# Smaller first loads, transposes in groups of six, thirteen raw rows and a two-piece last store in a fused layernorm and MLP

## The chip, the cores and the metric

The kernel runs on one core of a Trainium2 chip. The metric is the device time in microseconds of one execution. An execution is also profiled once; times within it are counted from the start of its span.

## The reference

```python
def reference(x, w1, b1, w2, b2):            # x [1, 2048, 1024], w1 [1024, 3584], w2 [3584, 1024], all bf16
    y = _layernorm(x, axis=-1)
    h = _gelu(jnp.einsum("bsd,df->bsf", y, w1) + b1)
    return jnp.einsum("bsf,fd->bsd", h, w2) + b2
```

Each of the 2048 tokens is normalised over its 1024 features (mean removed, divided by the root of the variance plus 1e-5), multiplied by w1, given b1 and a tanh gelu, multiplied by w2 and given b2.

## The kernel before

**Tiling.** The tokens are cut into 16 tiles of 128, four tiles to a block of 512 (`TB`), so there are four blocks. The first product is made transposed: a *row* r is 128 of the 3584 columns of w1 (28 rows, `FT`), and a row's result is a PSUM tile of 128 partitions by 512 tokens, summed over eight contraction blocks (`DT`). One matmul of a row and a contraction block is a *cell* (`pe_cell`, L415). A gelu on ScalarE (`act_gelu`, L424) takes the row from PSUM to `hT_sb`. The second product (`out_chunk`, L467) makes 128 tokens by 512 output columns as a sum of 28 matmuls; VectorE adds b2 (L478) and SP stores the piece. For each block TensorE runs the 28 rows and then eight output chunks.

**PSUM.** There are eight banks: `ps_t` (one bank, for transposes and for rows), `ps_1` (five banks, for rows) and `ps_2` (two, for the first rows, then for output chunks). `new_unit` gives a row its bank. Rows 0 to 6 of block 0 take 1_0 to 1_4, 2_1, 2_0; all later rows go round t, 1_0, 1_1, 1_2, 1_3, 1_4. The first cell in a bank waits for the gelu that last read the bank.

**Block 0 before its statistics are known.** The cells need the tokens transposed. For later blocks VectorE normalises and transposes (`ops_norm`, `ops_T`). For block 0 tiles 0 to 2 (`N_RAW`) are transposed on TensorE as they are (`pe_T`, L383), copied by ScalarE from PSUM to `yT_sb` (L391), and rows 0 to 6 (`R`, the *wave*) run on these raw values. A column of ones behind the 384 raw tokens (`RC`) gives the sum of each row's weights. VectorE takes the statistics (`op_stats`, L271, two halves of 512 features to a tile; `op_aggr`, L279), GpSimd the power -1/2 (L276, L498), and VectorE turns means and inverse roots into rows (`ops_rows`, L283 to L290; `ops_rvt`, L294) that TensorE spreads over the partitions (`pe_row`, L564) and ScalarE copies out (L567). `act_cs` (L531) copies the weight sums. VectorE then corrects each wave row in PSUM in two operations (`ops_corr`: `sa_r`, L540, and `sb_r`, L543). Tile 3 is normalised by VectorE before it is transposed on TensorE, and enters the wave rows as late cells of 128 columns (`late_cells`).

From row 7 on, the rows of block 0 use tokens that VectorE has *centred* (`ops_fix`, L339, one operation a tile, needing the row of means), 512 columns at a time, and VectorE only multiplies them by the inverse root (`dve_scale`, L548). In row 7 the last tile's 128 columns come first and the 384 behind them.

**Order.** Each engine runs its instructions in the order in which the program lists them. `_emit` puts a wait on a semaphore ahead of an instruction for each event it needs. The orders of TensorE and ScalarE are written by hand for the wave; VectorE's list begins with `head` (statistics, rows, norm of tile 3, b1, the three centrings), then the corrections, and the rest is merged from two lists: `crit` (work on PSUM, taken in the order it was appended) and `fill` (preparation of the next blocks), by estimated times that begin at `T_PE_START` and `T_DVE_START`.

**Loads.** SP issues `SP_FIRST_LOADS` and then all other loads; ScalarE issues `ACT_FIRST_LOADS` ahead of its table load. w0 to w7 are the eight contraction blocks of w1 for rows 0 to 6 (224 KB each), w8 and up the further rows. x0a, x1a and x2a are the first 512 features of a tile, xrb the other 512 of tiles 0 to 2. At the start TensorE runs `WARM` matmuls on constants (L491).

**End.** The last half tile of output is made in four pieces of 128 columns (`TAIL_PIECES`), each with its own add and store.

Of the kernel before, what the change touches and what calls it, by code (L numbers as in the profile page):

```python
# [18 lines left out]
TAIL_PIECES = 4  # L19
WARM = 24  # L20
N_RAW = 3
RC = N_RAW * P
HALVES = (0, 4, 8)
W1_CHUNK_COLS = (512, 512, 1024, 640)
N_W2_CHUNKS = 4
SP_FIRST_LOADS = ("x0a", "w0", "w1", "xrb", "w2", "w3", "w4", "x3a", "x3b", "w5", "w6", "w7", "b1", "w8")
ACT_FIRST_LOADS = ("x1a", "x2a")

T_PE_START = 4.2
T_DVE_START = 26.0  # L30
# [54 lines left out]
def bass_standalone__mixer_channel_mlp__prompt_kernel(  # L85
# [23 lines left out]
    assert HALVES[-1] == DT and 0 < N_RAW < TPB  # L109
# [27 lines left out]
    with ExitStack() as es:  # L137
# [25 lines left out]
        cs_sb = sb("cs_sb", [P, R], F32)  # L163
# [44 lines left out]
        def issue(item):  # L208
            if item == "xrb":
                dma(x_sb[:, 0:N_RAW, HC:D], xf[0:N_RAW * P, HC:D].rearrange("(t p) d -> p t d", p=P), item,  # L210
                    N_RAW * P * HC * 2)
                for i in range(N_RAW):
                    x_ev[i] = (f"x{i}_0", item)
            elif item[0] == "x" and item[-1] in "ab":
                i, h = int(item[1:-1]), "ab".index(item[-1])
                dma(x_sb[:, i, h * HC:(h + 1) * HC], xf[i * P:(i + 1) * P, h * HC:(h + 1) * HC], f"x{i}_{h}",
                    P * HC * 2)
                x_ev[i] = (f"x{i}_0", f"x{i}_1")
# [15 lines left out]
        for i in range(TPB):  # L234
            if i not in x_ev:
                load_x_tile(i)
            else:
                for h, evn in enumerate(x_ev[i]):
                    if evn not in est:
                        issue(f"x{i}" + "ab"[h])  # L240
# [29 lines left out]
        def op_stats(i, h):  # L270
            return (lambda e, i=i, h=h: e.bn_stats(st_sb[:, i, 6 * h:6 * (h + 1)], x_sb[:, i, h * HC:(h + 1) * HC]),  # L271
                    [x_ev[i][h]], f"st{i}_{h}", 0.65)
# [64 lines left out]
        def ops_fix(i):  # L337
            s0, s1 = i * P, (i + 1) * P
            return [(lambda e: e.tensor_tensor(out=yT_sb[:, 0, :, s0:s1], in0=yT_sb[:, 1, :, s0:s1],  # L339
                                               in1=row_sb[:, 0:1, s0:s1].to_broadcast([P, DT, P]), op=ALU.add),  # L340
                     ["row0", f"te{i}_0", f"te{i}_1"], f"fx{i}v", 1.25)]
# [4 lines left out]
        def ops_T(i):  # L346
            blk, t = divmod(i, TPB)
            waits = [y_ev[i][-1]]
            if blk - 2 in mm1_done:
                waits.append(mm1_done[blk - 2])  # L350
            elif blk == 1:
                waits += [f"cw_{R - 1}"] + list(FX)
# [13 lines left out]

        pe_t = [T_PE_START]
        bank_read = {}
        t_bank = {"t": ps_t[:, 0, :], "2_0": ps_2b[:, 0, :], "2_1": ps_2b[:, 1, :]}

        def pe_T(parts, bname):
            bap = t_bank[bname]
            nb = HALVES[1]
            last = f"tp{parts[-1][0]}_{parts[-1][1]}"
            w0 = ["ident"] + ([bank_read[bname]] if bname in bank_read else [])
            copies = []
            for n, (i, k) in enumerate(parts):
                j0, j1 = HALVES[k], HALVES[k + 1]
                buf, s0 = (1 if i < N_RAW else 0), i * P
                o = n * nb * P  # L380
                for j in range(j0, j1):
                    waits = (w0 if n == 0 else []) + [x_ev[i][k] if i < N_RAW else y_ev[i][j]] if j == j0 else []
                    pe.op(lambda e, i=i, j=j, o=o + (j - j0) * P: e.transpose(  # L383
                        out=bap[:, o:o + P], in_=x_sb[:, i, j * P:(j + 1) * P], identity=ident[:, :]),
                        waits=waits, sig=(f"tp{i}_{k}" if j == j1 - 1 else None))
                    yT_ev.setdefault(i, [None] * DT)[j] = f"te{i}_{k}"
                src = bap[:, o:o + (j1 - j0) * P].rearrange("p (j s) -> p j s", j=j1 - j0)
                copies.append((yT_sb[:, buf, j0:j1, s0:s0 + P], src, f"te{i}_{k}"))
                pe_t[0] += (j1 - j0) * 0.056
            for dst, src, sig in copies:  # L390
                act.op(lambda e, dst=dst, src=src: e.copy(out=dst, in_=src), waits=[last], sig=sig)  # L391
                bank_read[bname] = sig
# [104 lines left out]
        head = [op_stats(i, h) for h in range(2) for i in raw] + [op_aggr(i) for i in raw]  # L497
# [3 lines left out]
        head += [op_stats(N_RAW, 0), op_stats(N_RAW, 1), op_aggr(N_RAW)] + ops_rows() + ops_rvt() + ops_norm(N_RAW)  # L501
        for i in range(N_RAW + 1, TPB):
            head += [op_stats(i, 0), op_stats(i, 1), op_aggr(i)] + ops_norm(i)
        head += ops_b1()
        h = DT // 2
        FX = [f"fx{i}v" for i in raw]
        for i in raw:
            head += ops_fix(i)
        for o in head:
            dve_put(o)  # L510

# [15 lines left out]
        cs_ap, cs_ev, corr = {}, {}, []  # L527
# [10 lines left out]
        def ops_corr(r):  # L538
            ap = unit_bank(wave[r][0])[:, 0:RC + 1]
# [11 lines left out]

        def late_cells(t, rows, dts):
            for r in rows:
                for dt in dts:
                    last = t == TPB - 1 and dt == DT - 1
                    pe_cell(r, dt, 0, t * P, (t + 1) * P, wave[r][0], [cs_ev[r], yT_ev[t][dt]],
                            f"m1_0_{r}" if last else None, False, last, shared=True)
                    if last:
                        corr.extend(ops_corr(r))
                        act_gelu(r, 0, TPB, wave[r][0], f"sb_{r}", f"g_0_{r}")  # L560
                        hT_row[(0, r)] = f"g_0_{r}"
# [9 lines left out]

        first, most, every = range(NB1), [*range(NB1), R - 1], range(R)
        pe_T([(0, 0)], "t")
        pe_T([(1, 0)], "2_0")
        cells(first, (0,), 0, 1)
        pe_T([(2, 0)], "2_1")
        cells(first, (0,), 1, 2)
        cells((R - 1,), (0,), 0, 2)
        cells(most, (1,), 0, 2)
        cells((NB1,), (0, 1), 0, 2)  # L580
        pe_T([(0, 1), (1, 1)], "t")
        cells(every, (0, 1), 2, 3)
        cells(every, (2,), 0, 3)
        pe_T([(2, 1)], "t")
# [3 lines left out]
        cells(first, (DT - 1,), 0, 3)
        act_cs(ps_1, 0, NB1, False)
        last2 = range(NB1, R)  # L590
        cells(last2, (4,), 0, 3)
        pe_T([(3, 0), (3, 1)], "t")
        cells(last2, range(5, DT), 0, 3)
        act_cs(ps_2, NB1, R, True)
        r4 = R // 2 + 1
        late_cells(3, range(r4), range(h))
        pe_row(1)
        late_cells(3, range(r4), range(h, DT))
        late_cells(3, range(r4, R), range(DT))
        for o in corr:  # L600
            dve_put(o)

        def mm1_rows(b, r0):
            for r in range(r0, FT):
                mm1_row(b, r, ((N_RAW, TPB), (0, N_RAW)) if b == 0 and r == r0 else ((0, TPB),))

        mm1_rows(0, R)
        for b in range(NB):
# [11 lines left out]
            for st in range(TPB):  # L620
                for dh in range(DH):
# [4 lines left out]
                    if last and TAIL_PIECES > 1:  # L626
                        pw = NCH // TAIL_PIECES
                        for k in range(TAIL_PIECES):
                            out_chunk(b, st, c0 + k * pw, c0 + (k + 1) * pw, dh if k == 0 else f"{dh}p{k}", prev)
# [65 lines left out]
```

## Time and profile before

| what | value |
|---|---|
| median of 3 runs | 397.79 us (397.51 to 397.87) |
| profiled execution | 397.62 us, span 396.36 us |
| granted TensorE clock (mean of the records) | 1.000 |
| TensorE busy | 393.4 us (99%) |
| VectorE, ScalarE busy | 160.6 us (41%), 83.4 us (21%) |
| second product (L467) | 980 matmuls, 194.3 us |
| first product (L415) | 979 matmuls, 167.3 + 34.0 us |
| transposes on TensorE (L383) | 32 matmuls |

A line of the timeline has the start in us, the length in us, the engine, the line of the code, the operation, written tile <- read tiles, the shape and the number of instructions merged into it; in brackets the idle time before it and what ended it. The chain that ended last is followed back from the last instruction through whatever released each step. Matmuls overlap, so their pace is read from the distance of their starts.

### The profile page before, as it was taken

The page shows a single profiled execution, that of the slowest core. Times are in us where ns is not written, and L with a number is a line of the kernel's source. Part 1 is how long each engine was busy: PE and PEld are TensorE (multiplying, and loading weights), DVE is VectorE, ACT ScalarE, POOL GpSimd, SP SyncE. Part 2 cuts the span into 40 slices and gives each one's busy share as a digit, 9 for nine tenths or more (in the row PEclk, how much of TensorE's full clock was granted, in tenths as well). Part 3 has the DMA queues.
Part 4 walks back from the last instruction along what each step waited for, and adds up shares of the span by engine and source line. Part 5 has one row for each costly group of instructions (what it writes and reads, how often), then busy time and mean ns, then how long its engine had stood idle before and what let it go on. Part 6 is the DMA issues. An engine that isn't in the chain of part 4 may idle for free.

```text
span 396.4 us, 4688 instructions
## 1 busy us (share of the span) xinstructions
PE 393.4 (99%) x2017; PEld 187.8 (47%) x2017; DVE 160.6 (41%) x340; ACT 83.4 (21%) x125; POOL 9.8 (2%) x28
## 2 busy tenths in 40 slices
PE   8999999999999999999999999999999999999998
PEld 7744444444444444444444444444444444444447
DVE  5988889988999405987100000001100000001111
ACT  4373330000143342000023443100003334400000
POOL 2001100011000100000000000000000000000000
PEclk9999999999999999999999999999999999999999
DMA  7999940000000000000000000000000000000001
GB/s 272 361 378 386 387 155 13 28 26 14 28 0 0 2 0 2 27 14 27 26 13 2 0 0 2 13 13 28 21 20 13 0 2 0 0 15 26 13 28 28
DMA packets 17036, 23.64 MB, mean 60 GB/s; under 512 B 1656, under 2 KB 10744, under 8 KB 17016
## 3 DMA queue, kind: packets, MB, share of 16 engines
q1 hardware_dynamic: 16728, 23.08, 16.5%
q8 instruction: 16, 0.26, 0.3%
q10 hardware_dynamic: 288, 0.26, 0.2%
q14 instruction: 4, 0.03, 0.0%
HBM read 19.14 MB, written 4.19 MB: 59 GB/s over the span
## 4 chain that ended last, share of the span: by engine, by line
PE 98%; DMA 1%; SPq 0%; DVE 0%; issue 0%
PE ps L467 49%; PE ps L415 41%; PE ps_t L415 8%; DMA w_sb<-in_w_dram 1%; PE ps_t L383 0%; SPq L185 0%; PE ps_t L564 0%; DVE o_sb L478 0%
## 5 line engine op out<-in xcount | busy, mean ns | idle before, releaser
L467 PE MATMUL ps<-w_sb,hT_sb 128*128 128x512 bf16 (+1 forms) x980 | 194.3, 361 | 0.0
L415 PE MATMUL ps<-yT_sb,w_sb 128*128 128x512 bf16 (+4 forms) x827 | 167.3, 360 | 0.3 <-ACT yT_sb L391 0.3
L467 PEld LDWEIGHTS ps<-w_sb,hT_sb 128*128 128x128 bf16 x980 | 91.1, 98 | 102.8
L415 PEld LDWEIGHTS ps<-yT_sb,w_sb 128*128 128x128 bf16 x827 | 77.6, 98 | 85.5 <-ACT yT_sb L391 0.5
L424 ACT ACTIVATE hT_sb<-ps,b_sb 128x512 bf16<-128x512 f32 x94 | 64.4, 687 | 234.6 <-PE ps L415 217.2
L478 DVE TENSOR_TENSOR o_sb<-ps,b_sb 128x512 bf16<-128x512 f32 (+1 forms) x35 | 22.6, 646 | 198.3 <-PE ps L467 198.2
L359 DVE STREAM_TRANSPOSE yT_sb<-x_sb 32x256 bf16<-32x256 bf16 x192 | 83.7, 436 | 21.6 <-PE ps_t L415 18.6
L415 PE MATMUL ps_t<-yT_sb,w_sb 128*128 128x512 bf16 (+2 forms) x152 | 34.0, 368 | 0.0
L271 DVE BATCH_NORM_STATS2 st_sb<-x_sb 128x6 f32<-128x512 bf16 x32 | 21.1, 676 | 4.1 <-DMA x_sb<-in_x_dram 3.9
L415 PEld LDWEIGHTS ps_t<-yT_sb,w_sb 128*128 128x128 bf16 x152 | 14.5, 98 | 16.5
L424 ACT ACTIVATE hT_sb<-ps_t,b_sb 128x512 bf16<-128x512 f32 x18 | 12.4, 686 | 17.7 <-PE ps_t L415 14.6
L548 DVE TENSOR_TENSOR ps<-ps,row_sb 128x384 f32<-128x384 f32 x17 | 9.4, 565 | 4.7 <-PE ps L415 4.5
L276 POOL TENSOR_TENSOR rstd_sb<-mv_sb,nhalf 128x1 f32<-128x1 f32 x13 | 7.0, 542 | 116.1 <-DVE mv_sb L279 115.5
L299 DVE TENSOR_SCALAR x_sb<-x_sb,mv_sb,rstd_sb 128x1024 bf16<-128x1024 bf16 x13 | 7.0, 541 | 1.9 <-POOL rstd_sb L276 1.3
L540 DVE SCALAR_TENSOR_TENSOR ps<-row_sb,cs_sb,ps 128x385 f32<-128x385 f32 x7 | 4.3, 615 | 0.0
L391 ACT COPY yT_sb<-ps_t 128x512 bf16<-128x512 bf16 x6 | 3.3, 588 | 4.3 <-PE ps_t L383 4.3
L543 DVE TENSOR_TENSOR ps<-ps,row_sb 128x385 f32<-128x385 f32 x7 | 4.0, 567 | 0.2
L279 DVE BATCH_NORM_AGGREGATE mv_sb<-st_sb 128x2 f32<-128x15 f32 x16 | 3.3, 214 | 1.2
L339 DVE TENSOR_TENSOR yT_sb<-yT_sb,row_sb 128x1024 bf16<-128x1024 bf16 x3 | 3.5, 1222 | 0.1
L491 PE MATMUL ps<-const-bfloat16-1.0 128*128 128x128 bf16 x24 | 2.7, 309 | 0.8 <-PEq L680 0.8
L491 PEld LDWEIGHTS ps<-const-bfloat16-1.0 128*128 128x128 bf16 x24 | 2.5, 143 | 0.8 <-issue 0.8
L548 DVE TENSOR_TENSOR ps_t<-ps_t,row_sb 128x384 f32<-128x384 f32 x4 | 2.3, 564 | 0.9 <-PE ps_t L415 0.8
(36 smaller groups left out, 16.6 us busy)
## 6 DMA issues: line engine op xcount, KB each, us to landing
w_sb<-in_w_dram SPq DMA_DIRECT2D x4, 1792.0 KB, 18.2
out_dram<-o_sb SPq DMA_DIRECT2D x31, 128.0 KB, 1.7
x_sb<-in_x_dram SPq DMA_DIRECT2D x3, 1024.0 KB, 14.5
w_sb<-in_w_dram SPq DMA_DIRECT2D x2, 1024.0 KB, 8.5
w_sb<-in_w_dram SPq DMA_DIRECT2D x1, 2048.0 KB, 14.6
w_sb<-in_w_dram SPq DMA_DIRECT2D x8, 224.0 KB, 5.1
w_sb<-in_w_dram SPq DMA_DIRECT2D x1, 1280.0 KB, 15.9
x_sb<-in_x_dram SPq DMA_DIRECT2D x3, 128.0 KB, 5.0
```

The costliest lines, as they stand in the source:

```text
L271: return (lambda e, i=i, h=h: e.bn_stats(st_sb[:, i, 6 * h:6 * (h + 1)], x_sb[:, i, h * HC:(h + 1) * HC]), [x_ev[i][h]], f"st{i}_{h}", 0.65)
L276: pool.op(lambda e, i=i: e.tensor_tensor(out=rstd_sb[:, i:i + 1], in0=mv_sb[:, i, 1:2], in1=nhalf[:, i:i + 1], op=ALU.pow), waits=[f"mv{i} ...
L299: return (lambda e, i=i, c0=c0, c1=c1: e.tensor_scalar(out=x_sb[:, i, c0:c1], in0=x_sb[:, i, c0:c1], scalar1=mv_sb[:, i, 0:1], scalar2=rst ...
L359: res.append((lambda e, src=src, dst=dst: e.transpose(out=dst, in_=src), waits, (f"tr{i}" if lastop else None), 0.47))
L415: pe.op(lambda e: e.matmul(unit_bank(bank)[:, n0:n1], lhsT=w1_sb[:, dt, r * P:(r + 1) * P], rhs=yT_sb[:, buf, dt, n0:n1], start=start, sto ...
L424: act.op(lambda e, r=r, n0=n0, n1=n1, bank=bank: e.activation(out=hT_sb[:, r, n0:n1], in_=unit_bank(bank)[:, n0:n1], func=ACT.Gelu_apprx_tanh,
L467: pe.op(lambda e, st=st, ft=ft, c0=c0, c1=c1, bank=bank: e.matmul(ps_2[:, bank, 0:c1 - c0], lhsT=hT_sb[:, ft, st * P:(st + 1) * P], rhs=w2 ...
L478: crit.append((est[sig], (lambda e, ob=ob, c0=c0, c1=c1, bank=bank: e.tensor_tensor(out=o_sb[:, ob, c0:c1], in0=ps_2[:, bank, 0:c1 - c0], ...
L491: pe.op(lambda e: e.matmul(ps_1[:, 0, 0:P], lhsT=unit, rhs=unit, start=True, stop=True), waits=[gate] if gate else [])
L540: return [(lambda e: e.scalar_tensor_tensor(out=ap, in0=row_sb[:, 0, :], scalar=cs_ap[r], in1=ap, op0=ALU.mult, op1=ALU.add), [f"m1_0_{r}" ...
L543: (lambda e: e.tensor_tensor(out=ap, in0=ap, in1=row_sb[:, 1, :], op=ALU.mult), [f"sa_{r}", "row1"], f"sb_{r}", 0.56)]
L548: crit.append((est[wait_ev], (lambda e: e.tensor_tensor(out=ap, in0=ap, in1=row_sb[:, 1, 0:RC], op=ALU.mult), [wait_ev, "row1"], f"sc_{r}" ...
```

## The change

- First loads: x0p, x1p, x2p bring the first 256 features of tiles 0 to 2 (two contraction blocks); xq brings features 256 to 511 of the three tiles and xr the other 512. w0 is now issued by ScalarE, ahead of x2p. Tile 3 comes in one load.
- TensorE: 20 warm matmuls, three fillers (`FILL`) between the transposes of tile 0 and tile 1; the first two blocks are transposed a tile at a time, the other six blocks for the three tiles together, six transposes to a group, with one ScalarE copy of 384 columns for each block. Block 0 of the contraction runs a tile at a time, the others 385 columns at once.
- Rows 7 to 12 run on the raw tokens as well (`raw_row`): 385 columns, then 128 late columns behind the next raw row; they are corrected with the two operations of `ops_corr`, and their weight sums are copied one by one. Row 13 is now the first centred row, in two parts, with row 12's late cells between.
- VectorE: tile 3's statistics and norm come ahead of the rows of means; the three centrings stand behind the corrections of rows 3, 4 and 5. The gelus and the weight-sum copies of these rows are put on ScalarE in the order of estimated times.
- The last half tile of output is made in pieces of 384 and 128 columns.

```diff
-TAIL_PIECES = 4
-WARM = 24
+TAIL_PIECES = (384, 128)
+WARM = 20
+FILL = 3
+RAW_ROWS = 13
+CENTRE_BEHIND = (3, 4, 5)
-SP_FIRST_LOADS = ("x0a", "w0", "w1", "xrb", "w2", "w3", "w4", "x3a", "x3b", "w5", "w6", "w7", "b1", "w8")
-ACT_FIRST_LOADS = ("x1a", "x2a")
+SP_FIRST_LOADS = ("x0p", "x1p", "w1", "xq", "w2", "w3", "xr", "w4", "x3", "w5", "w6", "w7", "b1", "w8")
+ACT_FIRST_LOADS = ("w0", "x2p")
...
-        head = [op_stats(i, h) for h in range(2) for i in raw] + [op_aggr(i) for i in raw]
+        head = [op_stats(i, k) for k in range(2) for i in raw]
+        for i in range(N_RAW, TPB):
+            head += [op_stats(i, 0), op_stats(i, 1), op_aggr(i)]
+        head += [op_aggr(i) for i in raw]
...
-        head += [op_stats(N_RAW, 0), op_stats(N_RAW, 1), op_aggr(N_RAW)] + ops_rows() + ops_rvt() + ops_norm(N_RAW)
...
+        for i in range(N_RAW, TPB):
+            head += ops_norm(i)
+        head += ops_rows() + ops_rvt() + ops_b1()
...
-        for i in raw:
-            head += ops_fix(i)
...
+                        for o in ops_corr(r):
+                            crit.append((est[f"m1_0_{r}"], o, 0))
+                            t_corr[0] += o[3]
+                        act_late.append((t_corr[0], lambda r=r: act_gelu(r, 0, TPB, row_bank[r], f"sb_{r}", f"g_0_{r}")))
+                        bank_gelu[row_bank[r]] = hT_row[(0, r)] = f"g_0_{r}"
+                        if r in CENTRE_BEHIND:
+                            for o in ops_fix(CENTRE_BEHIND.index(r)):
+                                crit.append((est[f"m1_0_{r}"], o, 0))
+                                t_corr[0] += o[3]
...
+        def raw_row(r):
+            bank, uw = new_unit()
+            row_bank[r] = bank
+            for dt in range(DT):
+                pe_cell(r, dt, 1, 0, RC + 1, bank, (uw if dt == 0 else []) + [yT_ev[i][dt] for i in range(N_RAW)],
+                        f"cw_{r}" if dt == DT - 1 else None, dt == 0, False, shared=True)
+            cs_ap[r], cs_ev[r] = cs_sb[:, r:r + 1], f"cs_{r}"
+            act_late.append((est[f"cw_{r}"], lambda: act.op(
+                lambda e: e.copy(out=cs_sb[:, r:r + 1], in_=unit_bank(bank)[:, RC:RC + 1]), waits=[f"cw_{r}"],
+                sig=f"cs_{r}")))
...
+        pe_T([(0, 2, 0, 1)], "t")
+        warm(FILL)
+        pe_T([(0, 2, 1, 2)], "2_0")
+        cells(every, (0,), 0, 1)
+        pe_T([(0, 2, 2, 3)], "t")
+        cells(every, (0,), 1, 2)
+        cells(every, (0,), 2, 3)
+        pe_T([(2, 3, 0, 3), (3, 4, 0, 3)], "t")
+        cells(every, (1, 2), 0, 3)
+        pe_T([(4, 5, 0, 3), (5, 6, 0, 3)], "t")
+        cells(every, (3,), 0, 3)
+        cells(first, (4,), 0, 3)
+        pe_T([(6, 7, 0, 3), (7, 8, 0, 3)], "t")
+        cells(last2, (4,), 0, 3)
+        cells(every, (5,), 0, 3)
+        cells(first, (6, 7), 0, 3)
+        act_cs(ps_1, 0, NB1, False)
+        pe_T([(0, 4, 3, 4), (4, 8, 3, 4)], "t")
+        cells(last2, (6, 7), 0, 3)
+        act_cs(ps_2, NB1, R, True)
+        late_row(0)
+        late_row(1)
+        pe_row(0)
+        late_row(2)
+        late_cells(TPB - 1, (3,), range(DT // 2))
+        pe_row(1)
+        late_cells(TPB - 1, (3,), range(DT // 2, DT))
+        for r in range(4, R):
+            late_row(r)
...
+        for r in range(R, NR):
+            raw_row(r)
+            if r > R:
+                late_row(r - 1)
+        mm1_row(0, NR, ((N_RAW, TPB), (0, N_RAW)), between=lambda: (late_row(NR - 1), flush_act()))
+        mm1_rows(0, NR + 1)
```

More of the change, by code (lines that the diff above doesn't have):

```diff
@@ L18 @@
 NOB = 2
-TAIL_PIECES = 4
-WARM = 24
+TAIL_PIECES = (384, 128)
+WARM = 20
+FILL = 3
 N_RAW = 3
+RAW_ROWS = 13
+CENTRE_BEHIND = (3, 4, 5)
 RC = N_RAW * P
-HALVES = (0, 4, 8)
 W1_CHUNK_COLS = (512, 512, 1024, 640)
 N_W2_CHUNKS = 4
-SP_FIRST_LOADS = ("x0a", "w0", "w1", "xrb", "w2", "w3", "w4", "x3a", "x3b", "w5", "w6", "w7", "b1", "w8")
-ACT_FIRST_LOADS = ("x1a", "x2a")
-T_PE_START = 4.2
-T_DVE_START = 26.0
+SP_FIRST_LOADS = ("x0p", "x1p", "w1", "xq", "w2", "w3", "xr", "w4", "x3", "w5", "w6", "w7", "b1", "w8")
+ACT_FIRST_LOADS = ("w0", "x2p")
+T_PE_START = 4.27
+T_DVE_START = 17.5
 DMA_T0 = 2.1
@@ L108, in bass_standalone__mixer_channel_mlp__prompt_kernel @@
     assert NB1 + NB2 + 1 <= 8 and NB2 == 2
-    assert HALVES[-1] == DT and 0 < N_RAW < TPB
+    assert DT == 8 and 0 < N_RAW < TPB
+    QC = 2 * P
+    NR = max(R, min(RAW_ROWS, FT - 2))
     w1_chunks = [(j, j + 1, 0, R * P) for j in range(DT)]
@@ L162, in bass_standalone__mixer_channel_mlp__prompt_kernel @@
         row_sb = sb("row_sb", [P, 2, RC + 1], F32)
-        cs_sb = sb("cs_sb", [P, R], F32)
+        cs_sb = sb("cs_sb", [P, NR], F32)
         ps_t = ps("ps_t", [P, 1, 1024], BF16)
@@ L208, in issue @@
         def issue(item):
[L209 to L218, printed above, removed]
+            if item in ("xq", "xr"):
+                c0, c1 = (QC, HC) if item == "xq" else (HC, D)
+                dma(x_sb[:, 0:N_RAW, c0:c1], xf[0:N_RAW * P, c0:c1].rearrange("(t p) d -> p t d", p=P), item,
+                    N_RAW * P * (c1 - c0) * 2)
+            elif item[-1] == "p":
+                i = int(item[1:-1])
+                dma(x_sb[:, i, 0:QC], xf[i * P:(i + 1) * P, 0:QC], item, P * QC * 2)
+                x_ev[i] = ("xq", "xr")
             elif item == "b1":
@@ L233, in bass_standalone__mixer_channel_mlp__prompt_kernel @@
             issue(item)
[L234 to L240, printed above, removed]
         if "b10" not in est:
@@ L271, in op_stats @@
             return (lambda e, i=i, h=h: e.bn_stats(st_sb[:, i, 6 * h:6 * (h + 1)], x_sb[:, i, h * HC:(h + 1) * HC]),
-                    [x_ev[i][h]], f"st{i}_{h}", 0.65)
+                    [x_ev[i][h]] + ([f"x{i}p"] if i < N_RAW and h == 0 else []), f"st{i}_{h}", 0.65)
         def op_aggr(i):
@@ L340, in ops_fix @@
                                                in1=row_sb[:, 0:1, s0:s1].to_broadcast([P, DT, P]), op=ALU.add),
-                     ["row0", f"te{i}_0", f"te{i}_1"], f"fx{i}v", 1.25)]
+                     ["row0"] + sorted(set(yT_ev[i])), f"fx{i}v", 1.25)]
         yT_ev = {}
@@ L351, in ops_T @@
             elif blk == 1:
-                waits += [f"cw_{R - 1}"] + list(FX)
+                waits += [f"cw_{NR - 1}"] + list(FX)
             res = []
@@ L367, in bass_standalone__mixer_channel_mlp__prompt_kernel, with raw_ev, pe_T @@
         pe_t = [T_PE_START]
+        t_done = []
         bank_read = {}
         t_bank = {"t": ps_t[:, 0, :], "2_0": ps_2b[:, 0, :], "2_1": ps_2b[:, 1, :]}
-        def pe_T(parts, bname):
+        def raw_ev(i, j):
+            return f"x{i}p" if j * P < QC else "xq" if j * P < HC else "xr"
+        def pe_T(groups, bname):
             bap = t_bank[bname]
[L373 to L392, printed above, removed]
@@ new lines, in pe_T @@
+            waits = ["ident"] + ([bank_read[bname]] if bname in bank_read else [])
+            n, copies = 0, []
+            last = f"tp{len(t_done)}"
+            t_done.append(last)
+            blocks = [(g, j, i) for g, (j0, j1, i0, i1) in enumerate(groups) for j in range(j0, j1) for i in range(i0, i1)]
+            for g, j, i in blocks:
+                pe.op(lambda e, i=i, j=j, o=n * P: e.transpose(
+                    out=bap[:, o:o + P], in_=x_sb[:, i, j * P:(j + 1) * P], identity=ident[:, :]),
+                    waits=waits + [raw_ev(i, j) if i < N_RAW else y_ev[i][j]],
+                    sig=(last if n == len(blocks) - 1 else None))
+                waits = []
+                yT_ev.setdefault(i, [None] * DT)[j] = f"{last}_{g}"
+                n += 1
+                pe_t[0] += 0.056
@@ L394, in bass_standalone__mixer_channel_mlp__prompt_kernel @@
+            o = 0
+            for g, (j0, j1, i0, i1) in enumerate(groups):
+                w = (j1 - j0) * (i1 - i0) * P
+                dst = yT_sb[:, 1 if i1 <= N_RAW else 0, j0:j1, i0 * P:i1 * P]
+                src = bap[:, o:o + w].rearrange("p (j s) -> p j s", j=j1 - j0)
+                act.op(lambda e, dst=dst, src=src: e.copy(out=dst, in_=src), waits=[last], sig=f"{last}_{g}")
+                o += w
+                bank_read[bname] = f"{last}_{g}"
         crit = []
@@ L435, in y_waits, with mm1_row @@
             return [yT_ev[b * TPB + t][dt] for t in range(t0, t1)]
-        def mm1_row(b, r, parts=((0, TPB),)):
+        def mm1_row(b, r, parts=((0, TPB),), between=None):
             bank, uw = new_unit()
@@ L440, in mm1_row @@
             for k, (t0, t1) in enumerate(parts):
+                if k == 1 and between:
+                    between()
                 for dt in range(DT):
@@ L500, in bass_standalone__mixer_channel_mlp__prompt_kernel @@
                 waits=[f"mv{i}" for i in raw] + ["nhalf"], sig="rstdr")
-        head += [op_stats(N_RAW, 0), op_stats(N_RAW, 1), op_aggr(N_RAW)] + ops_rows() + ops_rvt() + ops_norm(N_RAW)
-        for i in range(N_RAW + 1, TPB):
-            head += [op_stats(i, 0), op_stats(i, 1), op_aggr(i)] + ops_norm(i)
-        head += ops_b1()
+        for i in range(N_RAW, TPB):
+            head += ops_norm(i)
+        head += ops_rows() + ops_rvt() + ops_b1()
         h = DT // 2
-        FX = [f"fx{i}v" for i in raw]
-        for i in raw:
-            head += ops_fix(i)
         for o in head:
             dve_put(o)
+        FX = [f"fx{i}v" for i in raw]
         wave = [new_unit() for _ in range(R)]
@@ L525, in cells @@
                 started.add(r)
-        cs_ap, cs_ev, corr = {}, {}, []
+        act_late, t_corr = [], [T_DVE_START]
+        cs_ap, cs_ev, row_bank = {}, {}, {r: wave[r][0] for r in range(R)}
         def act_cs(banks, r0, r1, flip):
@@ L538, in ops_corr @@
         def ops_corr(r):
-            ap = unit_bank(wave[r][0])[:, 0:RC + 1]
+            ap = unit_bank(row_bank[r])[:, 0:RC + 1]
             return [(lambda e: e.scalar_tensor_tensor(out=ap, in0=row_sb[:, 0, :], scalar=cs_ap[r], in1=ap,
@@ L550, in dve_scale, with late_row @@
             return f"sc_{r}"
+        def late_row(r):
+            late_cells(TPB - 1, (r,), range(DT))
         def late_cells(t, rows, dts):
@@ L555, in late_cells, with flush_act @@
                     last = t == TPB - 1 and dt == DT - 1
-                    pe_cell(r, dt, 0, t * P, (t + 1) * P, wave[r][0], [cs_ev[r], yT_ev[t][dt]],
+                    pe_cell(r, dt, 0, t * P, (t + 1) * P, row_bank[r], [cs_ev[r], yT_ev[t][dt]],
                             f"m1_0_{r}" if last else None, False, last, shared=True)
                     if last:
-                        corr.extend(ops_corr(r))
-                        act_gelu(r, 0, TPB, wave[r][0], f"sb_{r}", f"g_0_{r}")
-                        hT_row[(0, r)] = f"g_0_{r}"
+                        t_corr[0] = max(t_corr[0], est[f"m1_0_{r}"])
+                        for o in ops_corr(r):
[7 more added lines that the diff above has]
+                                t_corr[0] += o[3]
+        def flush_act():
+            for _, f in sorted(act_late, key=lambda a: a[0]):
+                f()
+        def raw_row(r):
[8 more added lines that the diff above has]
+                sig=f"cs_{r}")))
         def pe_row(k):
@@ L570, in pe_row @@
             pe_t[0] += _mm_us(RC)
[L572 to L584, printed above, removed]
@@ L585, in bass_standalone__mixer_channel_mlp__prompt_kernel @@
-        cells(every, (3,), 0, 3)
-        cells(first, range(4, DT - 1), 0, 3)
-        pe_row(0)
[L588 to L596, printed above, removed]
+        first, last2, every = range(NB1), range(NB1, R), range(R)
+        pe_T([(0, 2, 0, 1)], "t")
@@ L597, in bass_standalone__mixer_channel_mlp__prompt_kernel @@
+        cells(first, (6, 7), 0, 3)
[5 more added lines that the diff above has]
+        late_row(1)
+        pe_row(0)
+        late_row(2)
+        late_cells(TPB - 1, (3,), range(DT // 2))
         pe_row(1)
[L598 to L601, printed above, removed]
+        late_cells(TPB - 1, (3,), range(DT // 2, DT))
@@ L603, in mm1_rows @@
+        for r in range(4, R):
+            late_row(r)
         def mm1_rows(b, r0):
             for r in range(r0, FT):
-                mm1_row(b, r, ((N_RAW, TPB), (0, N_RAW)) if b == 0 and r == r0 else ((0, TPB),))
-        mm1_rows(0, R)
+                mm1_row(b, r)
+        for r in range(R, NR):
[4 more added lines that the diff above has]
+        mm1_rows(0, NR + 1)
@@ L625, in bass_standalone__mixer_channel_mlp__prompt_kernel @@
                     last = (b == NB - 1 and st == TPB - 1 and dh == DH - 1)
[L626 to L629, printed above, removed]
+                    if last:
+                        for k, pw in enumerate(TAIL_PIECES):
+                            out_chunk(b, st, c0, c0 + pw, dh if k == 0 else f"{dh}p{k}", prev)
+                            c0 += pw
                     else:
```

## The prediction

> **What bounds the kernel now.** I read the chain that ended last first, then TensorE's timeline of the first 22 us, then VectorE's and ScalarE's between 14 and 26 us, then the end.
>
> ```profile
> PE 98%; DMA 1%; SPq 0%; DVE 0%; issue 0%
> PE ps L467 49%; PE ps L415 41%; PE ps_t L415 8%; DMA w_sb<-in_w_dram 1%; PE ps_t L383 0%; SPq L185 0%; PE ps_t L564 0%; DVE o_sb L478 0%
> ```
>
> TensorE is the chain. After about 21 us it never waits, so only its instruction count, its waits in the first 20 us and the last store can move the time.
>
> ```profile
> 0.82 2.72 PE L491 MATMUL ps<-const-bfloat16-1.0 128*128 128x128 bf16 x24 [0.82 <-PEq L680]
> 3.51 0.58 PE L383 MATMUL ps_t<-ident,x_sb 128*128 128x128 bf16 x4
> 3.89 0.63 PE L383 MATMUL ps<-ident,x_sb 128*128 128x128 bf16 x4
> 4.77 0.64 PE L415 MATMUL ps<-yT_sb,w_sb 128*128 128x128 bf16 x5 [0.25 <-ACT yT_sb L391]
> 5.25 0.39 PE L383 MATMUL ps<-ident,x_sb 128*128 128x128 bf16 x4
> ...
> 13.41 0.32 PE L564 MATMUL ps_t<-rvt_sb,sel_sb 128*128 128x384 bf16 x1
> ...
> 17.19 2.40 PE L415 MATMUL ps<-yT_sb,w_sb 128*128 128x128 bf16 x40
> ```
>
> Starts are 0.107 us apart until 5.2 and 0.056 from 5.25 (40 in 2.40): the slow clock ends near 5.2. By then 8 transposes and 5 cells are done, so TensorE stands as if it had run dense and fast from 5.245 - 13 x 0.0557 = 4.52. Three waits follow: 0.23 (second weights, whose last part lands at 6.04), 0.14 (second halves of x, 7.07), 0.09 (the rows' matmul at 13.41): 0.46 in all.
>
> ```profile
> 14.28 3.50 DVE L339 TENSOR_TENSOR yT_sb<-yT_sb,row_sb 128x1024 bf16<-128x1024 bf16 x3
> 17.69 0.62 DVE L540 SCALAR_TENSOR_TENSOR ps<-row_sb,cs_sb,ps 128x385 f32<-128x385 f32 x1
> 18.35 0.57 DVE L543 TENSOR_TENSOR ps<-ps,row_sb 128x385 f32<-128x385 f32 x1
> 18.82 0.61 DVE L540 SCALAR_TENSOR_TENSOR ps<-row_sb,cs_sb,ps 128x385 f32<-128x385 f32 x1
> ...
> 26.04 1.49 DVE L548 TENSOR_TENSOR ps<-ps,row_sb 128x384 f32<-128x384 f32 x3
> ```
> ```profile
> 13.77 0.48 ACT L567 COPY row_sb<-ps_t 128x384 f32<-128x384 f32 x1 [3.25 <-PE ps_t L564]
> 17.39 0.48 ACT L567 COPY row_sb<-ps_t 128x384 f32<-128x384 f32 x1 [0.84 <-PE ps_t L564]
> 18.95 0.69 ACT L424 ACTIVATE hT_sb<-ps,b_sb 128x512 bf16<-128x512 f32 x1 [1.07 <-DVE ps L543]
> ```
>
> A raw row costs VectorE 1.125 us (17.69 to 18.82), a centring 1.14 (three from 14.28 to 17.69), a row from centred tiles 0.47 (L548). These give the term that decides.
>
> **Head.** w0 goes to ACT's queue, ahead of x2p; SP still issues 17 loads before w8, 0.47 apart, and the table load stays at 1.70 on ACT. From 20 warm matmuls TensorE is free at 0.82 + 20 x 0.107 = 2.96. The first x0p bytes move 1.2 us after issue, as x0a's did; it has half x0a's bytes, so it lands between 2.8 and x0a's 3.37; I take 3.0 (transposes at 3.15). Two transposes, three fillers, two of x1 end at 3.9. The copy of x0 (256 columns, 0.39; a 384 takes 0.48, a 512 0.59) is seen at 4.05; w0, issued 0.45 earlier than before (then landed at 4.55), should be there. Seven cells, two x2 transposes and two cells follow slowly until 5.2: 15 useful by 5.2, as if dense from 4.365. That is 0.15 gained. The 0.46 of old waits goes too: w1 is wanted at 6.4 instead of 5.86; halves become xq and xr; the rows are not needed until 16.9. New: x2's copy is seen at 5.70, its cells could start at 5.50: 0.20. xq: bytes asked up to it are 851 KB, what stood ahead of and in w1 before (852 KB; 15 of 16 parts at 5.2, the last 6.04), and it is wanted at 6.10: nothing, up to 0.5 if its 512-byte rows cost like 1024-byte ones. The Trainium skill ("DMA: Bandwidth & Descriptors", Queues, rings and completion order) has each DMA engine alternate between the two queues by packet, which speaks against w0 beside x; by the rows, x0a and x1a did land together (3.37 and 3.56), and it would put the range's upper end here, not the sum.
>
> **x3 and rows.** Eight weights fit a line (0.331 MB/us from 2.6 us): xr at 7.8 to 8.4, x3 at 9.3. VectorE: second statistics from 8.2, 1.9; x3 1.3; aggregates 0.7; x3's norm after POOL's 0.56 ends at 12.9; POOL now does rstd3 ahead of the rows' pow (0.88), so the row operations (2.52) run 13.25 to 15.8. TensorE transposes x3 at 14.45: covered. The last starts at 14.83; copies are seen 0.90 and 1.385 later (15.10 to 15.94 and 16.43 before, plus 0.055). Ahead of row 0's late cells stand only four cells (0.65; six before), and its fifth cell needs the second copy: 0.19 + 0.26 = 0.45 of waiting. So pe_row(0) starts at P0 = 16.9, a microsecond after its rows. pe_row(1) waits for row 0's copy: 0.36 + 0.48 + 0.055 = 0.893 after P0, against 0.83 of cells between: 0.06.
>
> **Raw rows 7 to 12.** Row 7 is 385 + 128 columns instead of 384 + 128; rows 8 to 12 get 8 more matmuls and columns each (0.023 x 5), row 13 is split (0.02): +0.14. In the wave 75 matmuls become 70: -0.01.
> Now the banks. Rows from 7 on take t and the five ps_1 banks in turn, so row 13 wants t again: its first cell waits for row 7's gelu. From P0 TensorE gets there after pe_row 0.163, rows 2 and 3 0.892, wait 0.06, pe_row 0.163, rows 4 to 6 1.337, six raw rows 7.83, late rows 7 to 11 2.23: P0 + 12.68. VectorE: row 0's copy at +0.84, sa_0 +0.87, sb_0 waits for row 1's copy, +1.77. Then seven pairs of 1.125 put sb_7's start at +9.65, but the centrings, which ran before the first pair, now stand behind rows 3, 4 and 5, ahead of row 7: 3 x 1.14, so +13.06. Its end (0.567), gelu (0.687), and latencies (0.09): +14.40. TensorE idles 14.40 - 12.68 = 1.72. Queued behind are late_row(12), row 13 and all else. Bounds 1.6 to 2.4 (unpipelined 1.18 and 1.22). ScalarE does not add: by its written order g1, cs7, g2, cs8, g3, cs9, g4, cs10, cs11, g5, cs12, g6, g7, it reaches g7 at +13.33 and waits. Other banks hold: row 8 needs g0 at +3.1 against +3.92; row 12 needs g4 at +8.8 against +10.9; row 14 needs g8 at +15.5 against +16.6. Block 1's preparation slides by some 4 us; its last transpose ended at 83.5 and is wanted at 104.2.
>
> **Tail.** 56 fewer matmuls, each 2.5 ns beside its columns (four of 128 take 223 ns, one of 512 takes 215.8): -0.14. The 384 piece's add and store issue end 0.5 before the last add; the last piece's 0.29 and store are unchanged.
>
> **Sum**, on the profiled 397.62 (span 396.36 + 1.26): -0.15 -0.46 +0.20 +0.45 +0.06 +0.14 -0.01 -0.14 +1.72 = +1.81, 399.43. The median of the runs shown is 0.17 above the profiled run; I take 399.5.
>
> **Rivals.**
> 1. VectorE's order is not what I read: were the centrings behind row 7, g7 would be 3.41 earlier (+10.99), ahead of TensorE's +12.68, and the wait gone: +0.09, 397.7. This is the not-slower case. It decides at 1.72 us less VectorE work ahead of row 7, or pairs of 0.88. For it: the merge of lists uses estimates. Against: the list is appended in that order, and seven pairs hold 1.125. With the clock early as well (next), 397.3 or less: 0.04 faster, 0.08 same.
> 2. Clock at another time. By the rows it rose 4.4 us after the first matmul; fewer warm-ups and gaps may move it. 1 us later costs 0.5, less the 0.2 of x2's copy; 1 us earlier gains up to 0.4: 399.0 to 399.9. The three runs are 0.36 apart. The Trainium skill ("TensorE: Matmul & The Clock Gate", Part 1) has a free-running window of 3.4 us, so the moment need not follow the first matmul; the trace's 4.4 agrees. 0.12.
> 3. Loads late: xq waits 0.5 and w0, crossing x0p and x1p, 0.3: 400.2. 0.10.
> 4. The idle 1.7 us lowers the clock again: 4.4 us at about half speed as at the start, 2.2 lost, 401.7. The profile of before has no idle over 0.5 to show it. 0.03. By the same page's rule of a whole idle window, 1.7 us would not do it.
> The forecast has 0.63.
>
> **Numbers.** Measurement can tell about 0.2% (0.8 us) from no change. Faster 0.04, same 0.08, slower 0.88. Range: the terms' low ends (stall 1.6, clock early -0.4, no x2 wait -0.2, -0.1 elsewhere) give 398.6; rival 3 with some of the stall's upper bound 400.5.
>
> **What would show it.** Right: an idle of about 1.7 us on TensorE near 29.6 us, ended by a gelu writing hT_sb, right ahead of a 128-column group on ps_t; two waits of 0.2 to 0.3 ended by copies of x3; corrections 1.125 apart with three centrings among them; first 512-column row at about 33.5 instead of 21.2 (six rows later). Wrong: no such idle, or three centrings behind the eighth pair, or TensorE short of work before pe_row(0) by over 0.5.

## The result

| | median | range |
|---|---|---|
| before (6 runs) | 397.76 us | 397.51 to 397.87 |
| after (6 runs) | 399.91 us | 399.75 to 400.31 |

The changed kernel is slower: ratio 1.0056, 95% interval 1.0043 to 1.0069, or 2.15 us. The forecast was 399.5 within 398.6 to 400.5. The profiled execution took 399.75 (span 398.5), 2.13 over the one of before; the sum had 1.81.

### The profile after

The chain that ended last, in order of time, around the place where the forecast put the loss (start, length, what; L416 is the cell, L425 the gelu, L378 the transpose, L593 `pe_row`, L470 the second product in the changed kernel's numbering):

```profile
22.59 0.45 PE ps_t L416 x8
23.03 6.58 PE ps L416 x56
...
29.65 0.62 DVE ps_t L544
...
30.30 0.58 DVE ps_t L547
...
30.90 0.69 ACT hT_sb L425
...
31.64 0.62 PE ps_t L416 x8
```

TensorE's chain breaks at 29.6. For 2 us it runs over VectorE and ScalarE: the two corrections of row 7 (they work on ps_t, which names the row) and row 7's gelu. The next TensorE piece is the first 128-column part of row 13, on ps_t. Before, nothing but TensorE stood in the chain from 17 us to the add ahead of the last store.

TensorE's timeline of the same kernel (in brackets the idle time and what ended it):

```profile
0.82 2.29 PE L494 MATMUL ps<-const-bfloat16-1.0 128*128 128x128 bf16 x20 [0.82 <-PEq L714]
3.64 0.37 PE L378 MATMUL ps_t<-ident,x_sb 128*128 128x128 bf16 x2 [0.52 <-DMA x_sb<-in_x_dram]
...
5.19 0.30 PE L378 MATMUL ps_t<-ident,x_sb 128*128 128x128 bf16 x2
...
6.36 0.50 PE L378 MATMUL ps_t<-ident,x_sb 128*128 128x128 bf16 x6
...
15.16 2.17 PE L416 MATMUL ps<-yT_sb,w_sb 128*128 128x385 bf16 x20
17.17 0.33 PE L593 MATMUL ps_t<-rvt_sb,sel_sb 128*128 128x384 bf16 x1
...
31.64 0.62 PE L416 MATMUL ps_t<-yT_sb,w_sb 128*128 128x128 bf16 x8 [1.60 <-ACT hT_sb L425]
```

The first transposes start at 3.64, 0.13 later than before, not 0.36 earlier. The four 385-column and sixteen 128-column cells from 15.16 would need 1.55 us and take 2.01 until pe_row(0) at 17.17: 0.46 of waiting for the copies of x3. The bracket of the last line is counted from the modelled end of the matmul before; from its start (29.825) plus one distance of 0.056 the wait is 1.76.

VectorE between the corrections (L544 and L547 are `sa` and `sb`, L334 a centring):

```profile
21.75 0.61 DVE L544 SCALAR_TENSOR_TENSOR ps<-row_sb,cs_sb,ps 128x385 f32<-128x385 f32 x1
22.40 0.57 DVE L547 TENSOR_TENSOR ps<-ps,row_sb 128x385 f32<-128x385 f32 x1
22.87 1.22 DVE L334 TENSOR_TENSOR yT_sb<-yT_sb,row_sb 128x1024 bf16<-128x1024 bf16 x1
24.00 0.62 DVE L544 SCALAR_TENSOR_TENSOR ps<-row_sb,cs_sb,ps 128x385 f32<-128x385 f32 x1
...
29.65 0.61 DVE L544 SCALAR_TENSOR_TENSOR ps_t<-row_sb,cs_sb,ps_t 128x385 f32<-128x385 f32 x1
30.30 0.57 DVE L547 TENSOR_TENSOR ps_t<-ps_t,row_sb 128x385 f32<-128x385 f32 x1
```

It never waits between 19.03 and 36; row 7's pair comes last of eight pairs and three centrings. TensorE had finished row 7's cells at 22.9, 6.8 us before VectorE reached them.

### The profile page after: what moved, and what is told of

Its sections match the earlier page's. It is cut to its first block, busy times and chain, and to the rows that moved or that the text cites. A ratio compares the mean times of both kernels' runs of the same rounds, so it can differ in the third digit from the quotient of the medians.

```text
span 398.5 us, 4682 instructions
## 1 busy us (share of the span) xinstructions
PE 393.5 (99%) x2003; PEld 188.4 (47%) x2003; DVE 163.6 (41%) x344; ACT 84.6 (21%) x134; POOL 9.9 (2%) x28
## 4 chain that ended last, share of the span: by engine, by line
PE 98%; DMA 1%; ACT 0%; DVE 0%; issue 0%; ACTq 0%
PE ps L470 49%; PE ps L416 41%; PE ps_t L416 8%; DMA x_sb<-in_x_dram 1%; PE ps_t L378 0%; ACT yT_sb L391 0%; ACT hT_sb L425 0%; DVE ps_t L544 0%; DVE ps_t L547 0%; PE ps_t L593 0%; PE ps L494 0%; DVE o_sb L481 0%; PE ps L378 0%; ACT cs_sb L535 0%; ACTq L74 0%
## 5 line engine op out<-in xcount | busy, mean ns | idle before, releaser
L470 PE MATMUL ps<-w_sb,hT_sb 128*128 128x512 bf16 (+2 forms) x924 | 194.1, 373 | 0.0
L416 PE MATMUL ps<-yT_sb,w_sb 128*128 128x512 bf16 (+3 forms) x862 | 168.4, 353 | 0.2
L470 PEld LDWEIGHTS ps<-w_sb,hT_sb 128*128 128x128 bf16 x924 | 89.3, 98 | 104.5
L416 PEld LDWEIGHTS ps<-yT_sb,w_sb 128*128 128x128 bf16 x862 | 79.8, 98 | 83.8 <-ACT yT_sb L391 1.1
L425 ACT ACTIVATE hT_sb<-ps,b_sb 128x512 bf16<-128x512 f32 x94 | 64.5, 687 | 232.1 <-PE ps L416 217.2
L481 DVE TENSOR_TENSOR o_sb<-ps,b_sb 128x512 bf16<-128x512 f32 (+2 forms) x33 | 22.3, 676 | 198.9 <-PE ps L470 198.8
L416 PE MATMUL ps_t<-yT_sb,w_sb 128*128 128x512 bf16 (+3 forms) x160 | 34.4, 358 | 1.6 <-ACT hT_sb L425 1.6
L416 PEld LDWEIGHTS ps_t<-yT_sb,w_sb 128*128 128x128 bf16 x160 | 15.0, 98 | 17.8 <-ACT hT_sb L425 1.8
L425 ACT ACTIVATE hT_sb<-ps_t,b_sb 128x512 bf16<-128x512 f32 x18 | 12.4, 687 | 17.1 <-PE ps_t L416 14.6
L552 DVE TENSOR_TENSOR ps<-ps,row_sb 128x384 f32<-128x384 f32 x12 | 6.8, 566 | 4.4 <-PE ps L416 4.0
L544 DVE SCALAR_TENSOR_TENSOR ps<-row_sb,cs_sb,ps 128x385 f32<-128x385 f32 x12 | 7.4, 615 | 1.8 <-ACT row_sb L596 1.8
L547 DVE TENSOR_TENSOR ps<-ps,row_sb 128x385 f32<-128x385 f32 x12 | 6.8, 567 | 0.6 <-ACT row_sb L596 0.2
L391 ACT COPY yT_sb<-ps_t 128x384 bf16<-128x384 bf16 (+2 forms) x10 | 4.4, 481 | 6.0 <-PE ps_t L378 6.0
L334 DVE TENSOR_TENSOR yT_sb<-yT_sb,row_sb 128x1024 bf16<-128x1024 bf16 x3 | 3.6, 1216 | 0.0
L378 PE MATMUL ps_t<-ident,x_sb 128*128 128x128 bf16 x30 | 2.8, 224 | 0.5 <-DMA x_sb<-in_x_dram 0.5
```

The lines of the kernel that those rows point to most:

```text
L416: pe.op(lambda e: e.matmul(unit_bank(bank)[:, n0:n1], lhsT=w1_sb[:, dt, r * P:(r + 1) * P], rhs=yT_sb[:, buf, dt, n0:n1], start=start, sto ...
L425: act.op(lambda e, r=r, n0=n0, n1=n1, bank=bank: e.activation(out=hT_sb[:, r, n0:n1], in_=unit_bank(bank)[:, n0:n1], func=ACT.Gelu_apprx_tanh,
L470: pe.op(lambda e, st=st, ft=ft, c0=c0, c1=c1, bank=bank: e.matmul(ps_2[:, bank, 0:c1 - c0], lhsT=hT_sb[:, ft, st * P:(st + 1) * P], rhs=w2 ...
L481: crit.append((est[sig], (lambda e, ob=ob, c0=c0, c1=c1, bank=bank: e.tensor_tensor(out=o_sb[:, ob, c0:c1], in0=ps_2[:, bank, 0:c1 - c0], ...
L544: return [(lambda e: e.scalar_tensor_tensor(out=ap, in0=row_sb[:, 0, :], scalar=cs_ap[r], in1=ap, op0=ALU.mult, op1=ALU.add), [f"m1_0_{r}" ...
L547: (lambda e: e.tensor_tensor(out=ap, in0=ap, in1=row_sb[:, 1, :], op=ALU.mult), [f"sa_{r}", "row1"], f"sb_{r}", 0.56)]
```

## The experiments

Each kernel was run beside the kernel before on the same chip. The measured totals carry a head (the time up to pe_row(0)) that varies by up to a microsecond from one profile to the next (17.17 to 18.15, last section), so each verdict also rests on a stretch that starts at pe_row(0): **D**, from the start of pe_row(0) to the first matmul of row 14. In the changed kernel D is 33.845 - 17.174 = 16.67. Where the record of a row's first matmul is missing, its start is taken as one distance ahead of the second.

### Row 13 in another bank

```diff
-            bank = first_ring[u] if u < len(first_ring) else ring[(u - len(first_ring)) % len(ring)]
+            if u < len(first_ring):
+                bank = first_ring[u]
+            elif u == NR:
+                bank = ("2", 1)
+            else:
+                bank = ring[(u - (1 if u > NR else 0) - len(first_ring)) % len(ring)]
```

> Row 13 takes bank 2_1, which row 5's gelu has left by 28.6 us, instead of bank t; everything else stays. Theory A (row 13 waits for row 7's gelu only because it wants bank t): the idle of 1.76 us ahead of row 13 goes, row 14 then takes t with nothing left to wait, and the time is 399.9 - 1.76 = 398.15. Rival B (ScalarE's written order, or the late cells, holds TensorE at that place whatever the bank): the idle stays at 1.5 or more, 399.9. Rival C (the wait moves to the next row that takes t): row 14 waits, 399 or more.

Measured: 398.52 (ratio to before 1.0018, 1.0008 to 1.0028). That is 0.86 over the kernel before beside it, where the changed kernel was 2.15 over its own: 1.29 less. The chain from 28 us:

```profile
27.91 4.88 PE ps L421 x51
32.80 0.05 issue
32.85 1.67 PE ps_t L421 x7
34.52 1.51 PE ps L421 x7
```

Rows 12, 13 and 14 follow each other with no other engine between them (row 14, on ps_t, shows x7 because the record of its first matmul is missing; the last line is row 15, cut off where the view ends). D is 32.63 - 17.73 = 14.90, 1.77 less: all of the wait, to 0.01. Nothing but banks was changed (row 13's, and so the place in the ring of the rows behind it), so theory A holds and B and C fall. The totals show less than 1.77 because the heads differ: in the profiled executions pe_row(0) started 0.56 later here, and 1.77 - 0.56 is the 1.21 by which the two profiled times differ (399.75 and 398.54).

### The centrings behind row 7

```diff
-                        if r in CENTRE_BEHIND:
-                            for o in ops_fix(CENTRE_BEHIND.index(r)):
+                        if r == R:
+                            for i in raw:
+                                for o in ops_fix(i):
```

> The three centrings stand together behind row 7's correction instead of behind rows 3, 4 and 5. Theory A: row 7's gelu comes 3.4 us earlier, ahead of TensorE, so the idle at row 13 goes; what is late next is the third centring for row 13's second part (0.16 us) and row 8's gelu for row 14 (0.55): 0.71 in place of 1.76, 398.85. Rival B (the centrings' place does not matter): 399.9 with the idle of 1.7 still ahead of row 13.

Measured: 399.10 (1.0035, 1.0022 to 1.0048). The chain from 28 us:

```profile
27.75 3.49 DVE yT_sb L334 x3
31.24 0.55 DVE ps L544
...
31.80 0.58 DVE ps L547
...
32.41 0.70 ACT hT_sb L425
33.10 0.27 issue
33.38 2.75 PE ps L416 x12
```

The wait at the start of row 13 is gone; its second part waits 0.23 for the third centring, and row 14 waits 0.48 for row 8's gelu: 0.71, as expected. D is 33.16 - 17.55 = 15.61. The total is 0.25 over the expectation, and pe_row(0) was 0.38 later. So it is VectorE's amount of work ahead of row 7 that sets the wait, and moving it pays only 1.06 of 1.76, since the centrings are wanted soon as well. The prediction's first rival, which had the centrings behind row 7, put the whole wait at nothing (397.7); it left out these 0.71.

### One raw row less

```diff
-RAW_ROWS = 13
+RAW_ROWS = 12
```

> Rows 7 to 11 run raw instead of 7 to 12, so row 12 (bank 1_4) is the first centred row and row 13 a whole one, still in bank t. Theory A: row 7's gelu comes when it came, row 13 waits 1.3 us for it, and since one row less stands behind the wait with split parts the time is 0.48 lower: 399.4. Rival B (the idle belongs to the first centred row, not to the bank): the idle moves to row 12 and stays near 1.7, 399.9.

Measured: 399.94 (1.0054, 1.0040 to 1.0067); the expected 0.48 is not in the median. In the trace it is:

```profile
32.84 1.67 PE L416 MATMUL ps_t<-yT_sb,w_sb 128*128 128x512 bf16 x7 [1.39 <-ACT hT_sb L425]
```

The wait sits ahead of row 13, which takes ps_t whole, and not of the first centred row 12; from the distance of the starts it is 1.34 (1.3 expected). D is 34.355 - 18.146 = 16.21, 0.46 less. In this execution (400.27) the head took it back: pe_row(0) came 0.97 later than in the changed kernel's profile. So the wait belongs to the bank, as the trace shows; a saving of half a microsecond is not shown in five totals.

### w0 behind x2p

```diff
-ACT_FIRST_LOADS = ("w0", "x2p")
+ACT_FIRST_LOADS = ("x2p", "w0")
```

> ScalarE issues x2p first and w0 behind it. Theory A (x0p landed at 3.50 us, later than the twice as long x0a did, because each of its packets took turns with a packet of w0): x0p lands by 3.2, the first transposes start by 3.35 instead of 3.64, and the time falls by 0.1 to 0.3, to 399.7, unless w0 comes after 4.5. Rival B (the landing is a latency that the neighbour does not set): x0p lands at 3.4 or later, and the later w0 makes the time 399.9 to 400.2.

Measured: 400.18 (1.0068, 1.0055 to 1.0081). Half of theory A holds: x0p lands at 2.90 instead of 3.50 and the first transposes start at 3.03 instead of 3.64. But w0 now lands at 4.33 instead of 3.82, and the cells start at 4.47, where they did:

```profile
3.03 0.37 PE L378 MATMUL ps_t<-ident,x_sb 128*128 128x128 bf16 x2
...
4.47 0.68 PE L416 MATMUL ps<-yT_sb,w_sb 128*128 128x128 bf16 x7 [0.34 <-DMA w_sb<-in_w_dram]
```

The total is the one that rival B gave. One profile against one would not settle it, since x0p's first packet moved at 2.10 in the changed kernel's profile and at 1.80 here. But in all seven profiles with w0 ahead of x2p, x0p landed at 3.34 to 3.53, and in the four of them whose first packet moved at 1.79 to 1.81 it landed at 3.34 to 3.48: about half a microsecond later than here. So the neighbour on the other queue sets when x0p lands, and what the one gains the other loses; that half microsecond agrees with the rule on alternating queues that the prediction weighed (the Trainium skill, "DMA: Bandwidth & Descriptors", Queues, rings and completion order). Later in the same execution TensorE waited 0.65 for xr.

### x3 transposed earlier

```diff
-        cells(first, (6, 7), 0, 3)
-        act_cs(ps_1, 0, NB1, False)
+        cells(first, (6,), 0, 3)
         pe_T([(0, 4, 3, 4), (4, 8, 3, 4)], "t")
+        cells(first, (7,), 0, 3)
+        act_cs(ps_1, 0, NB1, False)
```

> The transposes of x3 move ahead of the last contraction block of rows 0 to 4, so five more cells (0.82 us) hide their copies; the wait for bank t stays. Theory A (row 0's late cells wait 0.28 + 0.18 for the two copies of x3, and the wait at row 13 is counted from pe_row(0), so it moves with it): both waits go, pe_row(0) starts 0.45 earlier, the idle at row 13 stays 1.76 and the time is 399.45. Rival B (the wait at row 13 has its own clock, VectorE's, that does not move with pe_row(0)): the idle at row 13 grows by what the copies gave, 399.9.

Measured: 399.78 (1.0047, 1.0033 to 1.0061), 0.13 less than the changed kernel, not told from nothing in the totals. In the trace the 0.46 is gone: from the end of x3's transposes (14.81) to pe_row(0) (17.17) there are 9 cells of 385 and 16 of 128 columns, 2.36 us of work in 2.36. The head had started its first group of six 0.46 later, so pe_row(0) came when it did in the changed kernel. D is 33.85 - 17.17 = 16.68, with 1.76 ahead of row 13. As pe_row(0) did not move, this run alone does not tell theory A from rival B. The other profiles do: pe_row(0) starts at 17.17, 17.59 (w0 behind x2p), 17.58 (next experiment) and 16.63 (all three), and VectorE starts row 7's pair 12.48 later in each; in the first three the wait at row 13 is 1.76 or 1.77. VectorE had its rows ready at nearly the same time here and in the kernel with all three edits (16.38 and 16.33), and still row 7's pair starts 0.54 earlier there, as pe_row(0) does. So the wait moves with pe_row(0): theory A holds and rival B falls.

### xq wanted later

```diff
-        pe_T([(2, 3, 0, 3), (3, 4, 0, 3)], "t")
-        cells(every, (1, 2), 0, 3)
+        cells(range(3), (1,), 0, 3)
+        pe_T([(2, 3, 0, 3), (3, 4, 0, 3)], "t")
+        cells(range(3, R), (1,), 0, 3)
+        cells(every, (2,), 0, 3)
```

> Three cells of contraction block 1 go ahead of the first group of six transposes, so xq is wanted 0.49 later. Theory A (the changed kernel's head varies because xq lands anywhere between 5.9 and 7.3 and is wanted at 6.4): up to 0.5 less waiting for xq, 0.08 more for its copy, 399.6 in the median. Rival B (the late DMA engine delays what comes after xq as well): TensorE waits for xr or w2 instead, 399.9.

Measured: 399.90 (1.0054, 1.0041 to 1.0066): no gain. In its profile xq's last part lands at 6.90 and the group starts at 6.95, hardly waiting, but the next group then waits 0.21 for xr. That is rival B's picture; one profile does not settle how often.

### The three together

> Row 13 in bank 2_1, x3's transposes earlier, xq wanted later: the three waits taken away together. Theory A (they add): 399.9 - 1.76 - 0.45 - 0.2 = 397.5, level with the kernel before or 0.2 below it. Rival B (they cover each other): the waits come back behind one another and the time stays above 398.

The edits of the first, fifth and sixth experiment in one kernel. Measured: 397.86 (11 runs), ratio to before 1.0004, interval 0.9995 to 1.0013: level with the kernel before. It is 2.05 below the changed kernel, where 2.4 was expected; the third edit gave nothing alone. Its row 14, on ps_t, starts behind no wait:

```profile
31.53 1.89 PE L421 MATMUL ps_t<-yT_sb,w_sb 128*128 128x512 bf16 x8
```

D is 31.53 - 16.63 = 14.90, and the stretch from 14.26 to row 14 is without a wait but for the 0.06 ahead of pe_row(1). So bank t's wait (1.76) and x3's copies (0.46) are what made the change slower; with them gone the rest of it is worth nothing that can be measured.

### The short tail on the kernel before

```diff
-TAIL_PIECES = 4
+TAIL_PIECES = (384, 128)
```

> The kernel before with the last half tile as 384 + 128 and nothing else. Theory A: 56 matmuls less of 2.5 ns, 0.14 off, 397.55; the second product's last stretch is 0.14 shorter. Rival B (the last store is later because the 384 piece's store is in its way): same time or longer.

Measured: 397.67 (11 runs), ratio 0.9995, interval 0.9986 to 1.0003. The last stretch of the second product in the kernel before, then here, then the last adds here:

```profile
345.95 48.57 PE ps L467 x308
```
```profile
345.68 48.43 PE ps L467 x252
```
```profile
392.57 0.56 DVE L478 TENSOR_TENSOR o_sb<-ps,b_sb 128x384 bf16<-128x384 f32 x1 [3.86 <-PE ps L467]
394.13 0.29 DVE L478 TENSOR_TENSOR o_sb<-ps,b_sb 128x128 bf16<-128x128 f32 x1 [1.00 <-PE ps L467]
```

48.43 instead of 48.57: the 0.14 is in the trace. The larger add ends a microsecond ahead of the last, and from the start of the last add to the end of the span it is 1.80 us, against 1.81 before, so rival B falls. In the totals the median is 0.12 below that of the kernel before beside it, which is within the interval: neither this nor any other kernel here is shown to beat the kernel before.

## Why the prediction was right

Step by step, with the profiled executions (the first line is the time from which TensorE stands as if it had run dense and fast; it was 4.52 before):

| step | predicted | measured |
|---|---|---|
| useful matmuls on the slow clock | 4.37 (-0.15) | 4.61 (+0.08) |
| old waits for w1, x halves, rows | -0.46 | gone; but for x2's copy TensorE does not wait from 5.3 to 16 us |
| x2's copy | +0.20 | +0.24 |
| xq | 0 | 0 (5.93, wanted at 6.36) |
| x3's copies | 0.19 + 0.26 | 0.28 + 0.18 |
| ahead of pe_row(1) | +0.06 | +0.06 |
| columns and matmuls of the raw rows, wave | +0.14 - 0.01 | +0.15 (what is left of the 2.31 by which row 14 starts later) |
| row 13's bank | +1.72 | +1.76 |
| last half tile | -0.14 | 48.57 to 48.43: -0.14 |
| sum | +1.81 | +2.15; the profiled times differ by 2.13 |

The mechanism, its place and its price held, and that was not luck: row 13 waited for row 7's gelu, and the first experiment took away the bank alone and with it the whole wait. The second confirms the reason (three centrings ahead of row 7) and what is next behind it. Of the rivals, the first (VectorE's order not as read) fell to the timeline of VectorE, and the fourth (the clock falls in the idle) to the cells behind it: row 12's late cells follow at 0.056 from 32.10. The third (loads late) did not come about in this execution: x0p was late, but xq was not waited for; with one raw row less the wait for xq was 1.1 us.

The term that was mis-sized is the first of the sum, the head's -0.15. It rested on x0p landing at 3.0, since it is half as long as x0a. It landed at 3.50, later than x0a's 3.37, for the most part because w0 ran beside it, which the prediction named and put into the range but not into the sum; the experiment on the order of w0 and x2p shows it (2.90). Four transposes, seven cells and one more transpose were done when the clock rose, 12 instead of 15 (0.17), and it rose 0.07 later than taken: +0.08 instead of -0.15. That is 0.23 of the 0.32 by which the sum fell short; row 13 and x2's copy gave 0.04 each. Some readings of the prediction are a little off, and nothing hangs on them: SP issues 16 loads ahead of w8 and not 17, the bytes up to xq are 852 KB and not 851, and 0.17 on 399.43 is 399.60 where it took 399.5.

Rival 2, the clock at another moment, had too small a place in the forecast, though it did not decide. That the clock rose at 5.2 in the profiled execution, where the prediction had it, was luck: in three of the five profiles of the last section it rose 1.5 to 1.8 later. There pe_row(0), or in the third the first group of six, came 0.38 to 0.56 later; the rival's rule (0.5 for each microsecond, less 0.2) gives 0.55 to 0.7.

## What to carry to other kernels

Where a buffer is taken in a ring, the wait for it is set by the slowest engine's queue ahead of its last reader, so count that queue up to the reader, in its written order, against the writer's work up to the reuse. Work that is taken off an engine's front and put between such readers is not free because the engine is 41% busy: the share is an average, and here the engine had 12 us without a gap at the one place that counted. A saving below the head's own scatter has to be read from a stretch with fixed ends, not from totals.

## What was not expected of the hardware

**The clock's rise.** Five kernels have the same TensorE instructions up to 6.3 us: the changed one and those with the other bank, the later centrings, one raw row less and the earlier x3. In their profiles the distance of 128-column matmuls falls from 0.107 to 0.056 at these times:

| kernel | clock rises | xq's last part lands | first group of six starts | pe_row(0) starts |
|---|---|---|---|---|
| changed | 5.2 | 5.93 | 6.36 | 17.17 |
| other bank | 7.0 | 6.65 | 6.86 | 17.73 |
| centrings behind row 7 | 6.7 | 6.46 | 6.74 | 17.55 |
| one raw row less | 4.2 to 4.5 (TensorE waited there) | 7.28 | 7.33 | 18.15 |
| x3 earlier | 6.7 | 5.87 | 6.82 | 17.17 (with 0.46 less waiting before it) |

The last fourteen cells of contraction block 0 and the first group of six in two of these timelines: with the other bank (the clock late) and with one raw row less (the clock early, TensorE then stopped by xq):

```profile
5.35 1.71 PE L421 MATMUL ps<-yT_sb,w_sb 128*128 128x128 bf16 x14
6.86 0.56 PE L378 MATMUL ps_t<-ident,x_sb 128*128 128x128 bf16 x6
```
```profile
5.17 1.20 PE L416 MATMUL ps<-yT_sb,w_sb 128*128 128x128 bf16 x14
7.33 0.51 PE L378 MATMUL ps_t<-ident,x_sb 128*128 128x128 bf16 x6 [0.96 <-DMA x_sb<-in_x_dram]
```

The first matmul starts at 0.82, so the rise lies between 3.4 to 3.6 and 6.2 us after it, with the same instructions ahead of it; the late ones lie beyond the forecast's one microsecond either way. The granted clock in the profile does not show it (1.00 from 0 to 5 us and from 5 to 10 in the changed kernel), so the distance of the matmuls is the only sign, and that the clock is behind it is a reading of that. The Trainium skill ("TensorE: Matmul & The Clock Gate", Part 1) has a free-running window of 3.4 us that has to be busy. An estimate from it is that the rise comes one to two windows after the first matmul, 3.4 to 6.8 us; the five times lie in it. The same part of the Trainium skill puts the rise at around 4 us, give or take 0.5; the spread here is wider. In the one profile with an early rise TensorE then waited 1.12 us for xq, which landed late, so what an early rise is worth is not shown. What sets the phase no run here shows.

**Landing of the last part.** A load's 16 parts do not land together: xq's fifteenth part landed at 5.88 and the last at 5.93 in the changed kernel, at 6.13 and 6.65 with the other bank, at 6.76 and 7.28 with one raw row less. A place that a median landing covers is so not always covered.
